# First transforms due 0.3 of a period sooner, with the bias added out of PSUM and the inverse table copied in portions

## The chip, the cores and the metric

One core of one Trainium2 chip. The metric is the device time of one execution in microseconds (us). The kernel before took 607.15 us in the first three runs (604.29 to 610.09) and 606.58 us with the fourth that was run beside the changed kernel.

## The reference

Eight sequences of 3072 positions and 256 channels go through a filter in frequency space, and then through a gated two-layer network.

```python
# filter
X = np.fft.rfft(x, axis=1)
Yr = Xr @ w_r - Xi @ w_i + b_r
Yi = Xr @ w_i + Xi @ w_r + b_i
Y  = soft_threshold(Yr, 0.01) + 1j * soft_threshold(Yi, 0.01)   # [the two lines are written together]
y  = np.fft.irfft(Y, n=3072, axis=1)
# network, x = y, x_prev = y one position earlier
xk, xr = mu_k * x + (1 - mu_k) * x_prev, mu_r * x + (1 - mu_r) * x_prev
k = np.maximum(xk @ w_k, 0);  v = k * k @ w_v
out = v / (1 + np.exp(-(xr @ w_r)))
```

## The kernel before

A transform of 3072 positions is split into two steps of 96 and 32, so that each is a matmul with a small table. In between, the data is turned round through DRAM. Each batch from 2 on therefore makes two round trips (batches 0 and 1 get their first transforms in another way, and make only the second):

- **A**: first transforms (eight units, four stores `Adr<-A`), then a fetch in eight transfers `A<-Adr`, then middle transforms, filter and back transforms (`middle`).
- **V**: six back units give six stores `Vdr<-V` of four pieces each, then a fetch in four transfers `V<-Vdr`, then the last transforms (`last`).

The order of everything is decided when the program is built. Streams of units (tokens, values, first, middle, last, table) carry due times, and a small scheduler always takes the ready unit with the earliest due time. It keeps its own estimates (`done`, `free`, `WRITE_US`) of when things will be ready. So a due time moves not only TensorE's work but also the order in which SyncE issues DMAs, and SyncE issues in exactly that order.

```python
def store(k):                                     # first transforms, group q of batch b
    nc.sync.dma_start(out=Adr[b][:, 8*q:8*q+8, :], in_=a)
    ...
    if q == 3:
        at(k + WRITE_US, fetch)                   # the A fetch, as soon as the store should have landed

def evac(k):                                      # filter, unit u [first matmuls cut]
    e = copy(k, z, ps, 1.03, 1.22)                # ScalarE or VectorE, whichever is free sooner
    release(h, e)
    at(e, shrink)
def shrink(k):
    nc.vector.tensor_tensor(out=z, in0=z, in1=bias0 if u == 0 else bias, op=ALU.add)
    nc.vector.tensor_scalar(out=y, in0=z, scalar1=LAM, scalar2=-LAM, op0=ALU.min, op1=ALU.max)
    nc.vector.tensor_tensor(out=y, in0=z, in1=y, op=ALU.subtract)

def store(k):                                     # back transforms, unit u
    for cj in range(4):
        nc.sync.dma_start(out=Vdr[b][24*cj+4*u:24*cj+4*u+4].rearrange(...), in_=vt[32*cj:32*cj+32])
    if u == NU - 1:
        at(k + (3.0 if b == 0 else WRITE_US), fetch)   # the V fetch: four transfers

P = 71.5                                          # the planned period of one batch
for b in range(B):
    s = START + P * (b - 1)
    ...                                           # batches 0 and 1 are special
    else:
        fb += first(b, s - 0.9 * P, s - 0.2 * P)
        fa += middle(b, s, s + 0.5 * P)
        fc += last(b, s + 0.75 * P, s + 0.95 * P)
```

## Time and profile before

| | kernel before |
|---|---|
| time, median of 4 | 606.58 us (604.29 to 610.09) |
| span and mean TensorE clock of the profiled run | 604.4 us, 0.993 |
| busy TensorE / VectorE / ScalarE | 94% / 86% / 72% |
| period from batch to batch | 70.3 us, but 74.6 in batch 3 |

The page cuts the span into 40 equal slices; a digit is the busy share, or the granted clock, in tenths. Of the kernel before, TensorE and its clock:

```profile
PE   4977999999999999889999999999999999999996
...
PEclk9999999999999999989999999999999999999999
```

Only the start, the pair of eights (about 242 to 272 us) and the last slice are not full. The waits of TensorE and of SyncE's queue, each line giving who waits, for whom, us in total, times and the longest (`banks` are the PSUM banks that TensorE writes):

```profile
PE banks L525 <- DMA V<-Vdr: 5.5, 6, 2.1
PE banks L448 <- DVE Y L438: 4.5, 3, 3.1
```

```profile
SPq L472 <- DMA Vdr<-V: 9.4, 6, 4.6
```

TensorE's wait for V is the stall near 250 plus the start; the wait for Y (4.5 us) is all in batch 0. SyncE stands 9.4 us in all before a V fetch until the last V store has landed. Its issues in batch 2 (start, duration, what, how many):

```profile
171.99 1.85 SPq L461 DMA_DIRECT2D Vdr<-V  x4
174.57 0.32 SPq L290 DMA_DIRECT2D Adr<-A  x1
175.29 2.99 SPq L472 DMA_DIRECT2D V<-Vdr  x4
...
190.48 3.91 SPq L304 DMA_DIRECT2D A<-Adr  x8
```

The V fetch follows the sixth V store at once, and the A fetch comes 15 us later, when V is already home.

### The profile page before, as it was taken

How to read it: one execution, taken by the hardware profiler on the slowest of the kernel's cores; microseconds unless marked ns; L12 is line 12 of the kernel's file. 1: busy time of each engine (PE TensorE's matmuls, PEld its weight loads, DVE VectorE, ACT ScalarE, POOL GpSimd, SP SyncE). 2: the span in 40 equal slices, each digit the busy share in tenths (PEclk: the TensorE clock that was granted, in tenths of full speed). 3: DMA queues.
4: the chain of work that ended last, by engine and by line, in shares of the span. 5: the costliest groups of instructions: out<-in, count | busy, mean ns of one | idle time of the engine just before them, and what ended most of it. 6: DMA issues, size and time to landing. Idle time of an engine off the chain costs nothing.

```text
span 604.4 us, 12322 instructions
## 1 busy us (share of the span) xinstructions
PE 570.7 (94%) x4823; PEld 430.9 (71%) x4891; DVE 517.6 (86%) x839; ACT 436.3 (72%) x477; POOL 23.9 (4%) x53
## 2 busy tenths in 40 slices
PE   4977999999999999889999999999999999999996
PEld 3856766677767787667776777677776778776775
DVE  7677998789998899958988888979988889989983
ACT  6956986767776777567786768777787777667553
POOL 7001000000000000000000000000000000000000
PEclk9999999999999999989999999999999999999999
DMA  8945849864589555793569935785347834362224
GB/s 149 158 87 129 171 96 240 190 129 106 107 202 213 142 123 119 173 222 99 124 133 225 203 77 117 159 247 125 94 104 186 185 96 89 80 183 50 65 64 102
DMA packets 68878, 84.06 MB, mean 139 GB/s; under 512 B 9042, under 2 KB 53844, under 8 KB 68820
## 3 DMA queue, kind: packets, MB, share of 16 engines
q1 hardware_dynamic: 62916, 68.98, 45.8%
q0 software_dynamic: 5712, 14.03, 14.9%
q8 instruction: 38, 0.62, 0.4%
q10 hardware_dynamic: 192, 0.26, 0.2%
q14 instruction: 20, 0.16, 0.1%
HBM read 50.07 MB, written 47.19 MB: 161 GB/s over the span
## 4 chain that ended last, share of the span: by engine, by line
PE 80%; DMA 7%; DVE 5%; ACT 5%; issue 2%; SPq 1%; POOL 0%; ACTq 0%; POOLq 0%; DVEq 0%
PE banks L655 25%; PE banks L611 24%; PE banks L422 12%; PE banks L638 6%; DMA V<-Vdr 4%; PE banks L448 3%; PE banks L394 3%; PE banks L279 3%; PE banks L525 3%; ACT rl L617 2%; DMA Vdr<-V 2%; DMA xs<-in_x_dram 1%; ACT YT L226 1%; PE banks L352 1%; DVE Y L438 1%
## 5 line engine op out<-in xcount | busy, mean ns | idle before, releaser
L617 ACT ACTIVATE rl<-banks 128x1024 bf16<-128x1024 f32 x192 | 195.5, 1033 | 76.2 <-PE banks L611 75.2
L611 PE MATMUL banks<-xk,wk 128*128 128x512 bf16 x700 | 190.6, 379 | 5.3 <-ACT A L226 0.8
L655 PE MATMUL banks<-wv,k 128*128 128x256 bf16 x1536 | 183.4, 272 | 0.3 <-DVE k L623 0.3
L655 PEld LDWEIGHTS <-k 128*128 128x128 bf16 x1536 | 149.7, 98 | 30.3 <-issue 1.2
L623 DVE TENSOR_TENSOR k<-rl 128x1024 bf16<-128x1024 bf16 x192 | 131.1, 686 | 17.9 <-ACT rl L617 17.2
L611 PEld LDWEIGHTS <-wk 128*128 128x128 bf16 x768 | 73.0, 98 | 59.7 <-issue 3.5
L422 PEld LDWEIGHTS <-XT 128*128 128x128 bf16 x768 | 74.1, 98 | 17.2 <-issue 1.2
L422 PE MATMUL banks<-wr,XT 128*128 128x256 bf16 x384 | 73.3, 272 | 0.5 <-ACT YT L226 0.2
L422 PE MATMUL banks<-wi,XT 128*128 128x256 bf16 x384 | 73.3, 273 | 0.4 <-DVE XT L404 0.4
L589 DVE SCALAR_TENSOR_TENSOR xk<-diff,muk,YT 128x512 bf16<-128x512 bf16 x96 | 70.0, 745 | 0.5
L589 DVE SCALAR_TENSOR_TENSOR xr<-diff,mur,YT 128x512 bf16<-128x512 bf16 x96 | 68.9, 745 | 0.0
L666 DVE TENSOR_TENSOR o<-banks,rg 128x1024 f32<-128x1024 f32 (+1 forms) x49 | 58.7, 1197 | 5.8 <-PE banks L655 5.8
L226 ACT ACTIVATE YT<-banks 128x768 bf16<-128x768 f32 x60 | 46.4, 815 | 21.7 <-PE banks L525 19.0
L226 ACT ACTIVATE XT<-banks 128x1024 bf16<-128x1024 f32 (+2 forms) x46 | 44.9, 982 | 14.5 <-PE banks L394 14.3
L226 ACT ACTIVATE z<-banks 128x1024 bf16<-128x1024 f32 x38 | 38.9, 1024 | 22.0 <-PE banks L422 21.9
L638 PE MATMUL banks<-wrm,xr 128*128 128x256 bf16 x384 | 50.2, 274 | 1.7 <-ACT rl L617 1.5
L226 ACT ACTIVATE A<-banks 96x1024 bf16<-96x1024 f32 (+1 forms) x44 | 44.6, 1015 | 8.8 <-PE banks L279 6.7
L643 ACT ACTIVATE rg<-banks 128x1024 bf16<-128x1024 f32 x48 | 49.5, 1032 | 0.5 <-PE banks L638 0.5
L638 PEld LDWEIGHTS <-xr 128*128 128x128 bf16 x384 | 37.3, 98 | 12.4 <-issue 2.3
L226 ACT ACTIVATE V<-banks 128x1024 bf16<-128x1024 f32 x35 | 36.0, 1029 | 13.8 <-PE banks L448 9.8
L436 DVE TENSOR_TENSOR z<-z,bias 128x1024 bf16<-128x1024 bf16 x48 | 32.9, 686 | 9.5 <-ACT z L226 9.4
L525 PEld LDWEIGHTS <-V 96*128 96x128 bf16 x512 | 27.2, 98 | 13.5 <-DMA V<-Vdr 7.3
(100 smaller groups left out, 448.9 us busy)
## 6 DMA issues: line engine op xcount, KB each, us to landing
out_dram<-o SPq DMA_DIRECT2D x188, 128.0 KB, 2.3
xs<-in_x_dram POOLq DMA_DIRECT2D x32, 384.0 KB, 5.8
Vdr<-V SPq DMA_DIRECT2D x192, 64.0 KB, 1.8
V<-Vdr SPq DMA_DIRECT2D x32, 384.0 KB, 6.6
Adr<-A SPq DMA_DIRECT2D x24, 384.0 KB, 5.3
A<-Adr SPq DMA_DIRECT2D x48, 192.0 KB, 5.6
wk<-in_moe_w_k_dram POOLq DMA_DIRECT2D x1, 512.0 KB, 12.5
wv<-in_moe_w_v_dram POOLq DMA_DIRECT2D x1, 512.0 KB, 13.8
```

Of the source, the lines that this page charges most:

```text
L226: nc.scalar.activation(out, in_, AF.Copy, bias=0.0, scale=1.0)
L422: nc.tensor.matmul(o, lhs, w[:, c, :], start=(w is wr and c == 0), stop=(w is wi and c == NCD - 1))
L436: nc.vector.tensor_tensor(out=z, in0=z, in1=bias0 if u == 0 else bias, op=ALU.add)
L525: nc.tensor.matmul(pv[:, c, :, i, :], V2[b, n2 // 8][:, n2 % 8, 128 * c:128 * c + 128], FI, start=True, stop=True)
L589: nc.vector.scalar_tensor_tensor(out=m[:, c, :], in0=df[:, c, :], scalar=mu[:, c:c + 1], in1=yp[:, c, :], op0=ALU.mult, op1=ALU.add)
L611: nc.tensor.matmul(ps[:, 512 * f:512 * f + 512], wk[:, c, 128 * ff:128 * ff + 128], xk[:, c, :], start=(c == 0), stop=(c == NCD - 1))
L617: nc.scalar.activation(rl, ps, AF.Relu, bias=0.0, scale=1.0)
L623: nc.vector.tensor_tensor(out=k2, in0=rl, in1=rl, op=ALU.mult)
L638: nc.tensor.matmul(ps[:, 256 * q:256 * q + 256], xr[:, c, 128 * q:128 * q + 128], wrm[:, c, :], start=(c == 0), stop=(c == NCD - 1))
L643: nc.scalar.activation(rg, ps, AF.Sigmoid, bias=0.0, scale=1.0)
L655: nc.tensor.matmul(ps[:, 256 * q:256 * q + 256], K2[t][:, ff, 128 * q:128 * q + 128], wv[:, ff, :], start=(ff == 0), stop=(ff == NCF - 1))
L666: nc.vector.tensor_tensor(out=o[:, lo:hi], in0=ps[:, lo:hi], in1=rg[:, lo:hi], op=ALU.mult)
```

## The change

Its intent: shorten the start (the inverse table GI no longer stands in one piece before the first filter unit; a z that VectorE would copy and then add to is read from PSUM once), and take the first transforms of later batches out of the crowd around the V round trip.

```diff
                 def evac(k):
-                    e = copy(k, z, ps, 1.03, 1.22)
+                    a = max(k, free["act"]) + 1.13
+                    if max(k, free["dve"]) + 2.35 <= max(a, free["dve"]) + 1.8:
+                        nc.vector.tensor_tensor(out=z, in0=ps, in1=bs, op=ALU.add)
+                        ...                       # release the bank, then shrink
+                        return
+                    nc.scalar.activation(z, ps, AF.Copy, bias=0.0, scale=1.0)
+                    ...                           # then add on VectorE as before
@@ back transforms wait for their third of the table, not for all of it
-                needs = [("y", b, u), "GI"]
+                needs = [("y", b, u), ("GI", u // 2)]
@@
-            fb += first(b, s - 0.9 * P, s - 0.2 * P)
+            fb += first(b, s - 1.2 * P, s - 0.5 * P)
@@
-    tab += [Unit(18.0 + n, 0.5, ["G"], table_gi(n)) for n in range(3)]
+    tab += [Unit(22.0 + 4.0 * n, 0.5, ["G", ("xt", 0, n)], table_gi(n)) for n in range(3)]
```

More of the change, by code (lines that the diff above doesn't have):

```diff
@@ L427, in issue, with add @@
                 y = Y[u] = ym_pool.tile([128, 1024], BF16, name="Y")
+                bs = bias0 if u == 0 else bias
                 def evac(k):
-                    e = copy(k, z, ps, 1.03, 1.22)
+                    a = max(k, free["act"]) + 1.13
+                    if max(k, free["dve"]) + 2.35 <= max(a, free["dve"]) + 1.8:
+                        nc.vector.tensor_tensor(out=z, in0=ps, in1=bs, op=ALU.add)
+                        e = run_on("dve", k, 1.22)
+                        release(h, e)
+                        shrink(e)
+                        return
+                    nc.scalar.activation(z, ps, AF.Copy, bias=0.0, scale=1.0)
+                    e = run_on("act", k, 1.03)
                     release(h, e)
-                    at(e, shrink)
+                    at(e, add)
+                def add(k):
+                    nc.vector.tensor_tensor(out=z, in0=z, in1=bs, op=ALU.add)
+                    shrink(run_on("dve", k, 0.67) - 0.1)
                 def shrink(k):
-                    nc.vector.tensor_tensor(out=z, in0=z, in1=bias0 if u == 0 else bias, op=ALU.add)
                     nc.vector.tensor_scalar(out=y, in0=z, scalar1=LAM, scalar2=-LAM, op0=ALU.min, op1=ALU.max)
                     nc.vector.tensor_tensor(out=y, in0=z, in1=y, op=ALU.subtract)
-                    done["y", b, u] = run_on("dve", k, 1.8)
+                    done["y", b, u] = run_on("dve", k - 0.1, 1.13)
                 at(end, evac)
@@ L712, in evac @@
                                                 scalar2=None, op0=ALU.mult)
-                if n == 2:
-                    done["GI"] = e
+                done["GI", n] = e
             at(end, evac)
```

## The prediction

> **What bounds the kernel now.** I began with the summary page and its busy shares, and then cut the run into stretches.
>
> ```profile
> PE 570.7 (94%) x4823; PEld 430.9 (71%) x4891; DVE 517.6 (86%) x839; ACT 436.3 (72%) x477; POOL 23.9 (4%) x53
> ```
>
> ```profile
> core 0: us, PE busy (x) PEld busy (x) DVE busy (x) ACT busy (x) POOL busy (x), PEclk, DMA share, GB/s
> 0.00:80.00 80.00, 61.30 (x659) 50.70 (x662) 62.14 (x131) 60.72 (x72) 14.60 (x35) 0.98 0.69 132
> 80.00:240.00 160.00, 157.57 (x1289) 117.81 (x1308) 144.50 (x225) 117.67 (x128) 4.72 (x10) 1.00 0.69 155
> 240.00:265.00 25.00, 21.37 (x167) 14.86 (x168) 18.34 (x31) 15.30 (x18) 1.01 (x2) 0.93 0.76 192
> 265.00:600.00 335.00, 330.27 (x2714) 247.50 (x2756) 291.91 (x455) 242.64 (x262) 3.54 (x7) 1.00 0.55 129
> ```
>
> TensorE (PE) is the bound. From 80 to 240 it idles 2.4 us of 160, and from 265 to 600 4.7 of 335. Within its work it is dense: sixteen 256-column matmuls of one value unit take 1.75 us from start to start of the next unit. Only two places can give time: the first 80 us (18.7 idle) and 240 to 265 (3.6 idle, at clock 0.93). The second is the chain of waits, and TensorE's timeline, near 250:
>
> ```profile
> 243.28 7.49 DMA Vdr<-V
> ...
> 252.21 8.30 DMA V<-Vdr
> ```
>
> ```profile
> 252.76 1.91 PE L655 MATMUL banks<-wv,k 128*128 128x256 bf16 x16
> 256.72 0.34 PE L525 MATMUL banks<-FI,V 96*128 96x96 f16 x4 [2.05 <-DMA V<-Vdr]
> 257.94 0.34 PE L525 MATMUL banks<-FI,V 96*128 96x96 f16 x4 [0.87 <-DMA V<-Vdr]
> ```
>
> The last transforms (L525) of a batch need V, which makes a round trip through DRAM: six stores and then one fetch in four transfers. In the fourth batch (counted from 0: batch 3) the last piece of the last store took 7.49 us instead of the median 1.8, beside an x load issued at 243.65 and an A store issued at 244.44, both belonging to first transforms. The fetch then came late. Comparing the starts of successive units there with their usual durations, I count 5.35 us lost, waits and slow clock together. The other batches lose under 1 us here, so the slack of this round trip is a few us.
>
> **What the Trainium skill says.** (1) "VectorE: DVE Perf Modes", section "The perf-mode tier table": a bf16 `tensor_tensor` in SBUF runs in 2x mode, with any PSUM operand in 1x. The trace agrees: the add z<-z,bias takes 0.686 us, the gating product that reads PSUM (L666, same 128x1024) 1.219. (2) "DMA: Bandwidth & Descriptors", section "Anatomy of one DMA — SWDGE (gpsimd) path": DMA engines do not wait on semaphores; the wait is done by the issuing sequencer. So one waiting DMA holds up everything behind it on SyncE. The trace agrees:
>
> ```profile
> SPq L304 <- DMA Adr<-A: 35.3, 6, 7.5
> ```
>
> This is SyncE standing before the A fetch until the A stores have landed. (3) The same page, section "Queues, rings and completion order": each DMA engine consumes a row's descriptors in ring order. In the trace the `out` transfer issued at 120.62, right behind an A fetch, needs 7.46 us to land, where the median is 2.3. (4) "TensorE: Matmul & The Clock Gate", section "What's actually happening": after an idle window of about 3.4 us the clock halves. The trace agrees: after the 3.11 us idle before 43.16, four matmuls of L448 take 0.94 us instead of 0.60.
>
> **The change part by part.** I read the built order of instructions of the changed kernel against that of the kernel before; matmuls and DMAs are the same in number.
>
> *Bias from PSUM.* 27 of the 48 additions now read PSUM on VectorE; 21 keep the ScalarE copy. VectorE pays 27 x (1.22 - 0.69) = +14.3 us, but its 10 z copies go (-12.2), and its share of the other copies changes: V 13 to 5, A (of the first transforms) 11 to 6, YT 15 to 21, about -10 in all. ScalarE loses 17 z copies (-17.4) and gains 8 V, 5 A and others, about -9 net. Neither engine bounds, and TensorE rarely waits for either after 80 us, so in the steady stretch this is worth about 0.
>
> *Inverse table in portions.* Before, three GI copies stand together on ScalarE (20.85 to 23.72) before the first z. Now each comes before its use. In batch 0 VectorE takes all six biases from PSUM: 6 x (1.22 + 0.43 + 0.69) + 5 negations x 0.29 = 15.5 us, about the 15.7 that TensorE needs for six groups (0.44 + 1.74 + 0.44 each). Following the new order by hand from the first z at about 24, with the waits for a finished Y and for the negation that now stands behind the fifth Y, I arrive at the last back transform at 42 to 43, where it was 43.16. The gain is 0.5 to 1.5 us, plus perhaps 0.5 to 1 between 59 and 82, where z and the copies of the tokens compete on ScalarE. I take -1.5.
>
> *First transforms sooner.* The due times move by 0.3 x 71.5 = 21.5 us. The number of units does not change, and from batch 2 on nothing waited for A. So the gain can only be the 5.35 us near 250. The cost is in SyncE's order. Before: last V store, A store, V fetch, `out`, A store, A fetch. Now, for batches 2 to 6: A store, fifth V store, `out`, **A fetch of the next batch (8 transfers), sixth V store**, V fetch. The A fetch must wait for its A store, and the V round trip is behind it.
>
> Set F at the start of the last first-transform unit. In the new order TensorE has from there to the first last-transform unit: that unit, three more first units and two back units (6 x 0.44), five half value units (5 x 1.75) and ten key or gate units (10 x 0.87) = 2.6 + 8.75 + 8.7 = 20.1 us, each duration from TensorE's timeline in the steady stretch. So the first half of V is wanted at F + 20.1 and the other, one last unit (0.34) and one key unit later, at F + 21.3. Before, the sixth V store stood free and this was about 16 us from the last back unit; now it is 20.1 - 5.2 = 14.9.
>
> The DMA side is taken from batch 1 of the kernel before, the one place where an A fetch ran without a V fetch beside it: last first unit at 109.14, A store issued at 111.28, A fetch issued from
>
> ```profile
> 116.62 3.91 SPq L304 DMA_DIRECT2D A<-Adr  x8
> ```
>
> which is F + 7.5, and landed at 126.60, F + 17.5. The sixth V store is ready at about F + 7.2 but is issued behind the eight fetches and lands behind their data: about F + 18.5. Then the V fetch starts at about F + 18.8. With little beside it (batch 7, issued 530.25) the first two pieces landed after 5.3 us and all four after 7.9. So the first half is there at F + 24.1 and the rest at F + 26.7, perhaps 0.7 later since an x load is issued at about F + 15.5. TensorE loses about 27.4 - 21.3 = 6.1 us, less a little hidden, plus some half clock: about 6 per batch. Five batches: +30. Minus the 5.35 that the old stall cost, minus 1.5 of the start: +23.
>
> Sum: 607.15 + 23 = 630. I shade it to 627, since the rivals below are all lower.
>
> **The rivals.** (a) *Head gain only*: the V round trip keeps its time, since packets of the V store slip past the A fetch. Then -5.35 - 1.5 gives about 600. For it: the stores are small (64 KB), and before, a V store issued beside traffic mostly landed in 2 to 4 us. Against it: ring order, and the sequencer cannot even issue the store earlier. (b) *Half a stall*: A stores landed in 3.1 to 7.1 us; with the fast ones the A fetch starts at F + 5.5 and the loss is 3 to 4 per batch: 607.15 + 17 - 7 = 617. (c) *VectorE becomes the bound*: it is at 86% and gets a longer instruction on the path of PSUM. Against it: its total falls by about 8 us, and the shares between 80 and 600 leave room. It would add under 5 us. (d) *Contention makes it worse*: x loads, A stores and V stores meet; a V store took 7.49 us once. With 8 or 9 us per batch: 640 to 645.
>
> **Range and chances.** A gain of 2% would need 12 us, and all idle time of TensorE outside the first 80 us is about 10; so faster gets 0.03. Slower by 2% needs 619.3, a net stall of at least 3.8 us in each of five batches. I think that likely, since each link is read off a measured duration, but the sum of three DMA steps is uncertain by some 2.5 us per batch: 0.64. The rest, 0.33, is (a) and (b). Range 606 to 640.
>
> **What would show it.** Right: TensorE waits for V<-Vdr at the last transforms of batches 2 to 6, 3 us or more each; about five dips in PE's row, spaced by one period, with a lower clock after each; SyncE's sixth V store issued right after the eight A fetches; a period of about 76 us in place of 70.3 (gate units of the chain at 402.36 and 472.68); z<-banks,bias at about 1.22 us; last back transform of batch 0 at 42 to 43. Wrong: no wait at the last transforms, or V fetch issued within 5 us of the last back unit; then the time is near 600 and my reading of the queue has failed. If the waits are there but TensorE waits for VectorE in the steady stretch too, (c) holds.

## The result, and the profile after

| | before | after |
|---|---|---|
| median of 4 runs | 606.58 us | 639.43 us |
| lowest to highest | 604.29 to 610.09 | 638.27 to 643.15 |
| ratio of the fast runs | | 1.0547 (95%: 1.0479 to 1.0614) |
| span and clock of the profiled run | 604.4 us, 0.993 | 636.5 us, 0.973 |

The changed kernel is slower by 5.5%. Ratios here are the mean time of one kernel's fast runs over that of the other's of the same rounds, so not quite the ratio of the medians quoted.

The lines that answer to those of before, first the busy shares and then three stretches of the run (columns as in the prediction's view of the same kind):

```profile
PE 585.8 (92%) x4891; PEld 436.6 (69%) x4891; DVE 511.7 (80%) x822; ACT 430.6 (68%) x467; POOL 23.6 (4%) x53
...
PE   4967999999987999799996999989999799999997
...
PEclk9998999999997999979999899989999899999999
```

```profile
80.00:240.00 160.00, 151.48 (x1233) 111.46 (x1232) 131.86 (x203) 112.83 (x122) 5.17 (x10) 0.98 0.66 156
240.00:265.00 25.00, 25.00 (x183) 17.86 (x182) 23.70 (x34) 17.46 (x19) 1.01 (x2) 1.00 0.80 164
265.00:600.00 335.00, 316.70 (x2591) 233.51 (x2590) 270.88 (x426) 226.11 (x243) 3.17 (x6) 0.96 0.51 124
```

The one old dip near 250 is gone (25.00 busy of 25). In its place stand five new ones, one in each of the batches 2 to 6, each with a lower clock. The idle time of TensorE between 265 and 600 rose from 4.7 to 18.3 us, and the clock there fell from 1.00 to 0.96. What TensorE and SyncE wait for:

```profile
PE banks L538 <- DMA V<-Vdr: 28.2, 17, 3.6
```

```profile
SPq L485 <- DMA Vdr<-V: 25.0, 12, 4.2
```

So the wait for V rose by 22.7 us, and the wait of the V fetch for the V stores by 15.6. SyncE's issues in batch 2 of the changed kernel, in the same view as before:

```profile
171.53 2.67 SPq L474 DMA_DIRECT2D Vdr<-V  x4
...
176.13 4.09 SPq L304 DMA_DIRECT2D A<-Adr  x8
180.32 2.89 SPq L474 DMA_DIRECT2D Vdr<-V  x4
187.81 2.61 SPq L485 DMA_DIRECT2D V<-Vdr  x4
190.47 2.44 SPq L690 DMA_DIRECT2D out_dram<-o  x4
```

The eight A fetches now stand between the fifth and the sixth V store. The sixth store lands at 187.05 to 187.67, and only then can the V fetch go. TensorE's side of the same moment:

```profile
186.80 1.91 PE L668 MATMUL banks<-wv,k 128*128 128x256 bf16 x16
191.81 0.34 PE L538 MATMUL banks<-FI,V 96*128 96x96 f16 x4 [3.10 <-DMA V<-Vdr]
195.16 0.50 PE L538 MATMUL banks<-FI,V 96*128 96x96 f16 x4 [3.00 <-DMA V<-Vdr]
195.46 1.91 PE L624 MATMUL banks<-xk,wk 128*128 128x512 bf16 x4
```

Two waits of 3 us, and then work at half clock: the key unit at 195.46 takes 1.91 us, and 1.03 elsewhere.

To add it up I compare the starts of successive units around the last transforms with their usual durations; what is over I call the excess of that batch (waits and slow clock together).

| batch | 1 | 2 | 3 | 4 | 5 | 6 | 7 |
|---|---|---|---|---|---|---|---|
| excess before, us | 1.06 | 0.78 | 5.52 | 0.78 | 0.78 | 0.78 | 0.49 |
| excess after, us | 2.03 | 8.47 | 8.54 | 9.06 | 6.38 | 6.92 | 0.31 |
| first token of the batch (start of its first weight load), after minus before, us | +3.48 | +11.62 | +14.66 | +22.52 | +27.70 | +33.42 | +32.08 |

Batches 2 to 6 have 39.4 us of excess against 8.6, which is +30.7. The span grew by 32.1.

Beside the loss: the bias part did on the engines what the diff says. The group of the new addition in the changed kernel (count, busy us, mean ns of one, idle time before):

```profile
L434 DVE TENSOR_TENSOR z<-banks,bias 128x1024 bf16<-128x1024 f32 x27 | 33.1, 1224 | 20.1 <-PE banks L422 20.1
```

### The profile page after: what moved, and what is told of

The parts are those of the page before. It is cut to its first block, busy times and chain, and to the rows that moved or that the text cites. A ratio compares the mean times of both kernels' runs of the same rounds, so it can differ in the third digit from the quotient of the medians.

```text
span 636.5 us, 12383 instructions
## 1 busy us (share of the span) xinstructions
PE 585.8 (92%) x4891; PEld 436.6 (69%) x4891; DVE 511.7 (80%) x822; ACT 430.6 (68%) x467; POOL 23.6 (4%) x53
## 4 chain that ended last, share of the span: by engine, by line
PE 80%; DMA 11%; ACT 3%; DVE 3%; SPq 1%; issue 1%; POOL 0%; ACTq 0%; POOLq 0%; DVEq 0%
PE banks L668 25%; PE banks L624 24%; PE banks L422 11%; DMA V<-Vdr 8%; PE banks L651 6%; PE banks L538 4%; PE banks L461 3%; PE banks L394 3%; PE banks L279 3%; DMA Vdr<-V 2%; DMA xs<-in_x_dram 1%; ACT rl L630 1%; PE banks L352 1%; ACT V L226 1%; SPq L485 1%
## 5 line engine op out<-in xcount | busy, mean ns | idle before, releaser
L624 PE MATMUL banks<-xk,wk 128*128 128x512 bf16 x768 | 198.6, 386 | 0.0
L226 ACT ACTIVATE YT<-banks 128x768 bf16<-128x768 f32 x54 | 41.8, 812 | 49.7 <-PE banks L538 47.6
L602 DVE SCALAR_TENSOR_TENSOR xk<-diff,muk,YT 128x512 bf16<-128x512 bf16 x96 | 70.3, 747 | 0.3
L602 DVE SCALAR_TENSOR_TENSOR xr<-diff,mur,YT 128x512 bf16<-128x512 bf16 x96 | 70.2, 748 | 0.0
L538 PE MATMUL banks<-FI,V 96*128 96x96 f16 x512 | 37.5, 227 | 28.6 <-DMA V<-Vdr 28.2
L538 PEld LDWEIGHTS <-V 96*128 96x128 bf16 x512 | 31.6, 109 | 40.6 <-DMA V<-Vdr 34.7
L226 ACT ACTIVATE V<-banks 128x1024 bf16<-128x1024 f32 x43 | 44.0, 1023 | 22.5 <-PE banks L461 18.7
L651 PE MATMUL banks<-wrm,xr 128*128 128x256 bf16 x384 | 52.6, 283 | 0.0
L226 ACT ACTIVATE A<-banks 96x1024 bf16<-96x1024 f32 (+1 forms) x49 | 49.3, 1025 | 3.4 <-PE banks L352 2.0
L434 DVE TENSOR_TENSOR z<-banks,bias 128x1024 bf16<-128x1024 f32 x27 | 33.1, 1224 | 20.1 <-PE banks L422 20.1
```

Of the source, the lines that this page charges most:

```text
L226: nc.scalar.activation(out, in_, AF.Copy, bias=0.0, scale=1.0)
L434: nc.vector.tensor_tensor(out=z, in0=ps, in1=bs, op=ALU.add)
L538: nc.tensor.matmul(pv[:, c, :, i, :], V2[b, n2 // 8][:, n2 % 8, 128 * c:128 * c + 128], FI, start=True, stop=True)
L602: nc.vector.scalar_tensor_tensor(out=m[:, c, :], in0=df[:, c, :], scalar=mu[:, c:c + 1], in1=yp[:, c, :], op0=ALU.mult, op1=ALU.add)
L624: nc.tensor.matmul(ps[:, 512 * f:512 * f + 512], wk[:, c, 128 * ff:128 * ff + 128], xk[:, c, :], start=(c == 0), stop=(c == NCD - 1))
L651: nc.tensor.matmul(ps[:, 256 * q:256 * q + 256], xr[:, c, 128 * q:128 * q + 128], wrm[:, c, :], start=(c == 0), stop=(c == NCD - 1))
```

## The experiments

My theory: the due times alone make the loss, through the A fetch that now stands inside the V round trip. The rivals: the bias or table part costs something too; the delay is SyncE's order alone, or the sharing of the DMA engines; part of the loss is the halved clock after each wait. Kernels of one group ran on the same chip (experiments 1 to 8 on one, 9 to 12 on another). The kernel before ran beside them: 607.29 us (601.86 to 607.7, 7 runs) beside the first four, 606.17 us (602.44 to 608.91, 7 runs) beside the next four, 608.39 us (607.28 to 610.61, 11 runs) beside the last four.

### 1. The due times alone

```diff
 # the kernel before, with
-            fb += first(b, s - 0.9 * P, s - 0.2 * P)
+            fb += first(b, s - 1.2 * P, s - 0.5 * P)
```

> The kernel before with the sooner due times alone (first transforms 1.2 to 0.5 of a period ahead instead of 0.9 to 0.2). Its build has the same order on SyncE as the changed kernel: A fetch, sixth V store, V fetch. Theory 1 (queue order behind the A fetch is the whole loss): 635 to 643 us, a ratio of 1.05 to 1.06 over before, and waits of TensorE for V of 20 us or more in all. Theory 2 (the longer VectorE instruction that adds from PSUM is a good part of the loss): 615 to 625, ratio 1.015 to 1.03.

Measured: 644.09 us (640.39 to 646.89), ratio 1.0615 (1.0552 to 1.0678). The excess of batches 2 to 6 is 8.5, 9.0, 6.9, 7.6, 8.6. TensorE's waits:

```profile
PE banks L525 <- DMA V<-Vdr: 26.1, 17, 4.3
```

One line of the diff makes the whole loss. It is some 4 us slower than the whole change, but the intervals of the two ratios overlap; so the other two parts together do not make the loss, and whether they make it smaller is not clear from this run.

### 2. Everything but the due times

```diff
 # the changed kernel, with
-            fb += first(b, s - 1.2 * P, s - 0.5 * P)
+            fb += first(b, s - 0.9 * P, s - 0.2 * P)
```

> The changed kernel with the old due times: table in portions and bias from PSUM alone. Theory 1: within 1% of before, 601 to 610 us; one stall like the one near 250 may stay or go, worth 5 us. Theory 2: 620 or more, with TensorE waiting for VectorE between 80 and 600 us.

Measured: 608.25 us (600.42 to 614.03), ratio 0.9967 (0.9862 to 1.0072): no difference, with a wide spread. The run of 614.03 is slow and is left out of the ratio; the fast ones took 600.42, 607.79 and 608.72. The profiled run had a stall of 7.23 us in batch 3 and 2.45 in batch 5. So the old stall is not tied to one batch. Whether it falls in is probably what makes the spread; only the profiled run could be looked into.

### 3. The A fetch 10 us later in the plan

```diff
 # the changed kernel, with
-                        at(k + WRITE_US, fetch)
+                        at(k + WRITE_US + 10.0, fetch)
```

> The changed kernel in all but one thing: the A fetch is put into SyncE's order 10 us of the schedule's time later, which places it behind the V fetch, while the first transforms and their x loads and A stores stay as soon as in the changed kernel. Theory 1: the stalls go, 597 to 608 us. Rival (the bandwidth that the sooner x loads and A stores take, not the order, delays V): 620 to 640, hardly better than the change.

Measured: 601.58 us (601.36 to 607.8), ratio 0.9943 (0.9878 to 1.0008). SyncE's issues in batch 2 show the order that this gives:

```profile
181.97 1.83 SPq L474 DMA_DIRECT2D Vdr<-V  x4
185.31 1.72 SPq L485 DMA_DIRECT2D V<-Vdr  x4
...
189.72 9.16 SPq L304 DMA_DIRECT2D A<-Adr  x8
```

With the early due times kept and only the A fetch behind the V fetch, the excess of batches 2 to 6 is 0.4 to 0.8, and all of the 33 us is gone. The sixth V store lands within 1.8 to 2.1 us again, though x loads and A stores stayed early, so the rival of this run is out. The profiled run was the slow one of 607.8; it had a stall of 7.26 us in batch 1.

### 4. The A fetch issued by GpSimd

```diff
 # the changed kernel, with
-                            nc.sync.dma_start(out=A2[b, hf][32 * cj:32 * cj + 32],
+                            nc.gpsimd.dma_start(out=A2[b, hf][32 * cj:32 * cj + 32],
```

> The changed kernel with the A fetch issued by GpSimd instead of SyncE, at the same place of the schedule. The sixth V store then neither stands behind the A fetch on the sequencer nor in its ring, but the A fetch and the V fetch share the 16 DMA engines. If sequencer and ring order are what counts: V fetch issued within 6 us of the last back unit, 600 to 612 us. If sharing the engines is as bad as standing in line: 620 to 640 us.

Measured: 630.41 us (629.76 to 632.0), ratio 1.0397 (1.0348 to 1.0446). Batch 2, SyncE:

```profile
174.94 1.81 SPq L474 DMA_DIRECT2D Vdr<-V  x4
184.72 2.93 SPq L485 DMA_DIRECT2D V<-Vdr  x4
```

and GpSimd (what ended its wait is inferred by the profile; the A fetch waits for the A stores):

```profile
173.80 4.90 POOL L304 DMA_DIRECT2D A<-Adr  x8 [20.21 <-DMA Vdr<-V]
178.73 0.53 POOL L68 DMA_DIRECT2D xs<-in_x_dram  x1
```

The sixth V store is issued 5.4 us sooner than in the changed kernel, but the V fetch only 3.1 us sooner. The store's four pieces took 4.2 to 8.4 us to land, beside the A fetch issued from 173.80 on the other queue. Freeing SyncE and its queue gives back 9 of 33 us. So the order on SyncE is only a part. The likeliest reason for the rest is that the A fetch and the V store move through the same DMA engines at the same time. But the edit did one thing more: GpSimd also issues the x loads, and one of them now stood behind the A fetch, so it was issued at 178.73, beside the V store, where the changed kernel had it at 169.32. How much of the rest is due to this x load was not taken apart. The Trainium skill has the sharing on "DMA: Bandwidth & Descriptors", section "Issuing engines are not separate DMA queues": DMAs started by different engines run on the same 16 DMA engines and interleave, and issuing from several saves only sequencer time. This run agrees in so far as the V store, on a queue of its own, still took 4.2 to 8.4 us.

### 5. TensorE kept busy while it waits

```diff
 # the changed kernel, before the first last-transform matmul of batches 2 to 6
+                    for i in range(16 if 2 <= b <= 6 else 0):
+                        nc.tensor.matmul(ps[:, 0:512], big["wk"][:, 0, 0:128], big["wk"][:, 0, 0:512],
+                                         start=True, stop=True)
```

The products are overwritten and never used; the output stays correct.

> The changed kernel with sixteen 128x512 matmuls on weights, whose result is overwritten, put in front of the last transforms of batches 2 to 6: about 3.5 us of useless TensorE work inside each wait for V. The result stays right. If the halved clock after each wait is the rest of the stall (in the changed kernel 8 us lost per batch, of which under 5 in gaps): most half-speed stretches go, 622 to 630 us, although more work is done. If the loss is all waiting for V and the clock does not matter: 639 to 645.

Measured: 640.5 us (638.06 to 644.77), ratio 1.0575 (1.0527 to 1.0622): as slow as the changed kernel, and in the range written down for the theory that the clock does not matter; the other theory would have made it up to 17 us less. TensorE in batch 2 of this run:

```profile
189.73 3.62 PE L533 MATMUL banks<-wk 128*128 128x512 bf16 x15
193.18 0.34 PE L541 MATMUL banks<-FI,V 96*128 96x96 f16 x4
194.59 0.34 PE L541 MATMUL banks<-FI,V 96*128 96x96 f16 x4 [1.08 <-DMA V<-Vdr]
...
196.61 0.34 PE L541 MATMUL banks<-FI,V 96*128 96x96 f16 x4 [0.81 <-DMA V<-Vdr]
197.69 0.99 PE L541 MATMUL banks<-FI,V 96*128 96x96 f16 x12 [0.73 <-DMA V<-Vdr]
```

The useless work fills the first wait almost exactly (3.45 of 3.10 us). Of half clock in batches 2 to 6 there remain three stretches of 3.4 us, where the changed kernel had four of 6.8 and one of 3.4. Still nothing is gained: the later pieces of V are now waited for at full clock. My reading is that the slow clock mostly ran beside a wait that would have been there anyway. In four of the five batches the first wait had been shorter than 3.45 us (2.06 to 3.10), so they lost a little to the useless work itself; a gain of about 1 us a batch could hide here, but not the 9 to 17 us of the other theory.

### 6. First transforms sooner still

```diff
 # the changed kernel, with
-            fb += first(b, s - 1.2 * P, s - 0.5 * P)
+            fb += first(b, s - 1.4 * P, s - 0.7 * P)
```

> The changed kernel with the first transforms due still sooner, 1.4 to 0.7 of a period ahead. Now the A fetch stands after the second V store of a batch and is over before the sixth. If it is the A fetch's place in the V round trip that costs: no waits of 3 us for V in batches 2 to 6, 598 to 610 us. If sooner first transforms as such cost (buffers, contention, more copies early): slower than the change, 640 or more.

Measured: 615.5 us (614.33 to 617.18), ratio 1.0141 (1.0112 to 1.0171), between the two ranges written down. Now the A fetch of batch 3 is issued at 166.21, before the last four V stores of batch 2 (from 173.87). Batches 2 to 6 have an excess of only 0.7 to 0.8 and periods of about 71 us. What remains is at the start: a stall of 8.63 us in batch 1, and one wait of 5.9 us for an output bank. So it is no law that sooner is worse. What matters is on which side of the V round trip the A fetch falls.

### 7. Late fetch, and batch 2 at its old due times

Experiment 3 left a stall in batch 1, where the first transforms of batch 2 had moved. This kernel leaves those where they were.

```diff
 # experiment 3, with
-            fb += first(b, s - 1.2 * P, s - 0.5 * P)
+            fb += first(b, s - 0.9 * P, s - 0.2 * P) if b == 2 else first(b, s - 1.2 * P, s - 0.5 * P)
```

> The run with the later A fetch, and batch 2's first transforms back at the old due time, because in that run's profile batch 1 still lost 7 us at its last transforms. If the six first transforms moved into the start-up are what delays V of batch 1: no run at 607, 597 to 601 us, faster than both kernels by some 1%. Otherwise the same as that run, 601 to 608.

Measured: 600.3 us (599.78 to 600.71), ratio 0.9888 (0.9865 to 0.9912). No stall in any batch (excess 1.07 at most), span 598.7, clock 0.994. It beats both kernels, and its runs lie within 1 us of each other.

### 8. Early due times and late fetch without the other two parts

```diff
 # the kernel before, with
-            fb += first(b, s - 0.9 * P, s - 0.2 * P)
+            fb += first(b, s - 1.2 * P, s - 0.5 * P)
-                        at(k + WRITE_US, fetch)
+                        at(k + WRITE_US + 10.0, fetch)
```

> The kernel before with the sooner due times and the later A fetch, without the table in portions and without the bias from PSUM. If those two parts are worth about nothing: within 0.5% of the run that has them too (601.6 median), 599 to 607. If the bias from PSUM helps: 607 to 615. If it hurts: under 599.

Measured: 606.95 us (605.95 to 608.25), ratio 1.0 (0.9972 to 1.0027). As in experiment 3, batches 2 to 6 run without a stall, but batch 1 has 5.45 us, and the start is as slow as in the kernel before (4.5 us of waiting for Y). The range for parts worth nothing reached to 607, and the intervals of experiments 3 and 8 overlap, so this run only hints that the bias and table parts together are worth something. The last three runs took this apart.

### 9. The late fetch alone

```diff
 # the kernel before, with
-                        at(k + WRITE_US, fetch)
+                        at(k + WRITE_US + 10.0, fetch)
```

> The kernel before, with only the A fetch due 10 us later and the first transforms due as before. If the late fetch alone makes the gain of the 600.3 us kernel (theory: it takes the A fetch out of the V round trip, and the stall of batch 3 with it): 600 to 603 us, no stall over 2 us at the last transforms of any batch. If the earlier first transforms are needed too (rival: a late fetch at the old due times brings A too late for the middle transforms, or the store's piece of 7.49 us in batch 3 comes from elsewhere): 606 or more, with a stall left in batch 3 or a wait for A.

Measured: 606.99 us (605.39 to 610.94), ratio 0.9984 (0.9959 to 1.0009): a miss. The stall of batch 3 is gone as expected (0.90), but the periods from batch 2 on became 71.1 us, where they were 70.3. (The first token also came 2.1 us later, but TensorE's matmuls up to there are the same in the same order, and such a difference is within the scatter of single runs; see the start, below.) TensorE's waits from 270 to 480 us, some three batches:

```profile
PE banks L638 <- ACT rl L617: 1.3, 3, 0.4
PE banks L394 <- ACT rl L617: 1.1, 3, 0.4
PE banks L611 <- ACT A L226: 0.8, 3, 0.3
PE banks L638 <- ACT A L226: 0.8, 3, 0.3
```

These are short waits for PSUM banks that ScalarE has not emptied: 4.0 us here, 1.7 in the same stretch of the kernel before and 1.4 in that of experiment 12. I read it so that the later fetch reshuffled the A copies and the network's copies on ScalarE for the worse. The late fetch alone is therefore not enough for the gain of experiment 7. Which of the other parts it needs is open: the early due times without the bias part gain nothing either (experiment 10 below, where a moved A fetch costs 5.4 us), and the late fetch with the bias part at the old due times was not run.

### 10 to 12. The table and the bias, each alone, where no stall hides them

```diff
 # 10: the kernel before, with the due times and the late fetch of experiment 7
 # 11: experiment 7, with the bias part undone (the table part stays)
 # 12: experiment 7, with the table part undone (the bias part stays)
```

> The kernel of 600.3 us without the table part and without the bias part. The prediction worked the table at -0.5 to -1.5 us and the bias at about 0: 600.5 to 602.5 us. Rival, that the two together are worth more where no stall hides them: 604 or more. If they are worth nothing: within 1 us of 600.3.

> The kernel of 600.3 us without the bias part alone. By the prediction the bias is worth about 0 in the steady stretch and lets batch 0 keep up: within 1.5 us of 600.3. Rival: ScalarE and VectorE together are tight enough that the bias part is worth over 2 us.

> The kernel of 600.3 us without the table part alone. By the prediction this costs 0.5 to 1.5 us, all before the last back transform of batch 0: 600.8 to 601.8 us, with that transform later than 43.2. Rival: nothing, since the fifth Y and not the table sets that transform: within 0.5 us of 600.3.

| | without the bias part | with it |
|---|---|---|
| whole table | (10) 607.92 us, 0.9989 (0.997 to 1.0007) | (12) 599.32 us, 0.986 (0.984 to 0.988) |
| table in portions | (11) 610.7 us, 1.0028 (1.0011 to 1.0046) | (7) 600.3 us, 0.9888 (0.9865 to 0.9912) |
| last back transform of batch 0, whole table | 42.99 | 41.93 |
| the same, table in portions | 46.75 | 43.28 |

The table part makes that transform later by 1.35 us with the bias part and by 3.8 without. Without the bias part the whole kernel is 2.8 us slower for it, and the intervals are apart; with it, 1.0 us, which is not clear of noise (experiments 7 and 12 ran on different chips, and their intervals overlap). Both ranges written down for experiment 12 missed: it came out faster, not slower or the same. The bias part is worth 8.6 us in the first row (607.92 minus 599.32), and I had expected 0. Of these, 5.4 us are not its arithmetic: without the bias part, in experiments 10 and 11 alike, the plan came out with the A fetch of batch 2 behind one more A store, so in experiment 10 it was issued at 126.47 and not at 118.22. The middle transforms of batch 2 wait for it, and the period from batch 1 to batch 2 is 75.4 us instead of 70.0. TensorE's waits between 128 and 205 us of experiment 10:

```profile
PE banks L377 <- DMA A<-Adr: 3.9, 1, 3.9
```

Another 2.4 us lie before that (the first token of batch 1 is at 130.1 against 127.7). Whether these are the bias part's is not shown: the kernel before, also without it, has that token at 127.4. TensorE at the end of batch 0's back transforms in experiment 12:

```profile
41.93 0.60 PE L461 MATMUL banks<-Y,GI 128*128 128x256 bf16 x4 [1.73 <-DVE Y L451]
```

and of experiment 10:

```profile
42.99 1.03 PE L448 MATMUL banks<-Y,GI 128*128 128x256 bf16 x4 [3.11 <-DVE Y L438]
```

A z that VectorE reads out of PSUM leaves ScalarE alone, and the last back transform starts 1.06 us sooner. Experiment 12 has the lowest median, 1.4% under the kernel before in the same rounds.

## Why the prediction was right or wrong

**The class and the size.** Slower by over 2% was right. The time was 639.43 against 627, inside the range of 606 to 640 by only 0.6 us. That it did not fall outside is luck: the sum below was 9.1 us too small.

**"A fetch of the next batch (8 transfers), sixth V store": right.** The order on SyncE is the one predicted, in batches 2 to 6, and experiments 1 and 3 show that it is the loss: one line brings it, and moving the A fetch alone takes it away. The period, foretold at about 76 us, came at 75.5 to 78.2.

**The chain from F**, the start of the last first-transform unit. In batch 2, F is 168.31:

| step | predicted | measured |
|---|---|---|
| A fetch issued | F + 7.5 | F + 7.8 |
| sixth V store landed | F + 18.5 | F + 18.7 to 19.4 |
| V fetch issued | F + 18.8 | F + 19.5 |
| first half of V there | F + 24.1 | F + 26.8 |
| all of V there | F + 26.7 to 27.4 | about F + 28.9 |
| first half of V wanted | F + 20.1 | F + 20.1 to 20.4 |

The four steps down to the issue of the V fetch hold within 0.9 us. The term that was mis-sized is "the first two pieces landed after 5.3 us and all four after 7.9". These came from batch 7, the one batch with little traffic beside it. In batch 2 of the changed kernel the second piece took 7.3 us from the start of the fetch, and all about 9.4, with an x load from 184.10 and `out` transfers from 190.47 beside them. I gave the x load 0.7 us for that. TensorE's two waits there, 3.10 and 3.00 us, are both for the first half of V. So "about 6 per batch" was 7.9 on average (39.4 / 5), and net of the usual 0.8 about 7.1. Rival (d), 8 or 9 us per batch from contention, lies nearer to what came.

**"Minus the 5.35 that the old stall cost."** It went as predicted: the stretch from 240 to 265 is full. But the size was that of one profiled run. Experiment 2, another kernel with the old due times, had 7.23 us there and 2.45 in batch 5, so 5.35 need not be the share of the median. Nor do the x load and the A store that I named beside the slow piece explain it by themselves: in batches 2, 4 and 5 of the same run they follow the last piece at the same distance (0.3 to 0.5 and 1.1 to 1.3 us), and there it landed in 1.8 us.

**"Ring order, and the sequencer cannot even issue the store earlier."** This was a part of the reason. Experiment 4 took both away and got back 9 of 33 us. For the larger part, that the V store and the A fetch share the DMA engines is likely, but not shown alone, since an x load came between as well. The time came out near because the step that I took from the trace (landing "behind their data") covers both.

**"Plus some half clock."** The half clock came, with stretches of 6.8 us in four of the five batches. Experiment 5 gives no sign that it is a separate term of the sum: with most of it gone, the time is the same, though a gain of about 1 us a batch could hide there. The prediction also calls its trace in agreement with an idle window of about 3.4 us; the idle that it names was 3.11 us, and in the changed kernel 2.06 us in batch 5 were enough.

**The start, "I take -1.5": not borne out.** The last back transform of batch 0 came at 43.41, not 42 to 43, and the first token was 2.25 us later than before. But single runs scatter as much. Seven profiled kernels have both the table and the bias part and the same matmuls in the same order up to the first token (the changed one and experiments 2 to 7): they start that transform at 42.47 to 43.69, and have the first token at 65.9 to 68.2. The five with neither part have 42.99 to 43.86, and 65.6 to 68.0. So the two parts together move the start by less than the scatter. The step that failed is "the gain is 0.5 to 1.5 us" from copying the table in portions: it shows in neither pair of kernels that differ by this part alone. The transform at 46.75 (experiment 11, table alone) and at 41.93 (experiment 12, bias alone) lie outside the scatter, and the table cost 2.8 us of time without the bias part and 1.0, not clear of noise, with it. In the trace of the changed kernel the negation of the fifth group stands behind the fifth Y on VectorE, and TensorE waits 2.1 us for it and then 2.1 us for the last Y. I had written down both waits, but had worked them too short.

**The bias part, "worth about 0": wrong by some 3 us, in the good direction.** The 3 us are the 8.6 less the 5.4 of the moved A fetch. The counts and the 1.22 us were right. What I had not seen is that it shortens batch 0, where TensorE waits for VectorE's Y: 3.11 us in experiment 10, 1.73 in experiment 12. Where the rest of the 3 us lies is not shown. It may be why experiment 1 (644.09) is slower than the whole change (639.43). That the bias part also moved an A fetch, worth 5.4 us between experiments 10 and 12, is an accident of the plan in those kernels.

**The sum.** From +23 before shading to the +32.1 of the span: the stalls made +30.7 where I had 30 - 5.35 = 24.65, which is 6.1 more, and the start made +2.25 in these two profiled runs, scatter included, where I had -1.5, which is 3.8 more. Together 9.9, and the rest (-0.8) is spread over the other stretches. The shading from 630 to 627 went the wrong way.

**Rivals (a), (b) and (c)** are out: V was waited for in all five batches, for over 6 us of excess each, and TensorE's waits for VectorE after 80 us are under 1 us each.

What stays open: why in some kernels with old due times a V store needs 5.0 to 7.5 us in batch 3 or 5, and in other batches with the same transfers beside it not. How far the halved clock would count if the V pieces came early together was not tried either.

## What to carry to other kernels

When due times, priorities or buffers are moved in a planned kernel, read the new issue order of the DMA queue first, and ask of each round trip through DRAM what now stands between its last store and its fetch; here a fetch of eight transfers there cost some 7 us a batch, and giving it another queue saved only 9 of 33 us. Size such a step with a transfer that ran beside the same traffic, not with the cleanest one in the trace. And try the good half of a change with the bad half repaired: here the early due times with a late fetch and the bias part gave 599.3 us, where the whole change had given 639.4.

## What the Trainium skill lacked or had wrong

- "DMA: Bandwidth & Descriptors", section "Queues, rings and completion order": nothing there or on another page says how much a small store slows down beside a large fetch. Here the four 64 KB pieces of a V store landed in 1.8 us in the median of the kernel before, in 4.8 to 6.7 us behind eight A transfers on the same queue, and in 4.2 to 8.4 us beside them (and an x load) from another queue.
- The same page, section "Issuing engines are not separate DMA queues": it calls the time saved on the sequencer "usually small relative to the DMA itself". Experiment 4 came out 9 of 33 us better, some 1.8 us for each of five batches: small beside a fetch of 7 us or more, but not in the sum, since on SyncE the sixth V store stood behind the eight A transfers. (The run frees the sequencer and the ring together and does not part the two.)
- "TensorE: Matmul & The Clock Gate", section "What's actually happening": it names an idle window of about 3.4 us before the halving, but not how idle the window must be. In the changed kernel the 3.41 us before each of the six halvings between 50 and 510 us hold 2.06 to 3.08 us of idle TensorE, and never 3.4. And the halving cost little by itself here: filling the first wait of each batch with useless matmuls (experiment 5) left 640.5 us against 639.4.
